# Fewer loads at the end of a decode attention kernel, and another home for the last 64 rows of the down projection

## The chip, the cores and the metric

One Trainium2 chip, one NeuronCore of it. The metric is the device time of one execution in microseconds; lower is better. Each kernel is run several times and the median is given. The profile is one more execution, taken by the hardware profiler; its span runs from the first to the last instruction. Names of engines: PE is TensorE (PEld its weight loads), DVE is VectorE, ACT is ScalarE, POOL is GpSimd, SP is SyncE, which issues nearly all DMAs here.

## The reference

One token of a conditioned transformer block: adaptive layer norm, attention of 32 heads over a cache of 16384 keys each, and a SwiGLU feed-forward layer, all in bfloat16.

```python
# A_x (1,1,640); A_k_cache, A_v_cache (1,32,16384,128); A_wq (640,4096); A_wo (4096,640)
# B_w_gate, B_w_up (640,1728); B_w_down (1728,640); c (1,640); w_mod (640,3840)
def A_ref(x, k, v, wq, wo):
    q = (x @ wq).reshape(1, 1, 32, 128).transpose(0, 2, 1, 3)
    p = softmax(einsum('bhqd,bhkd->bhqk', q, k) * 128 ** -0.5)
    return einsum('bhqk,bhkd->bhqd', p, v).transpose(0, 2, 1, 3).reshape(1, 1, 4096) @ wo

def B_ref(x, w_gate, w_up, w_down):
    return silu(x @ w_gate) * (x @ w_up) @ w_down

sa, ca, ga, sb, cb, gb = split(silu(c) @ w_mod, 6)
x = x + ga * A_ref(layernorm(x) * (1 + ca) + sa, k, v, wq, wo)
out = x + gb * B_ref(layernorm(x) * (1 + cb) + sb, w_gate, w_up, w_down)
```

The two caches are 268 of the 290 MB that are read.

## The kernel before

The 32 heads are worked in 16 pairs (NP = 16). A pair's K is 8 MB, laid out as 128 partitions (two heads times 64) with 256 keys of 128 numbers each; its V likewise. K goes to one of the two slots of `kring`, V to `vbuf`; the V of the last pair (PL = 15) goes to slot 0 of `kring`, because `vbuf` is wanted for wo.

Every operation is entered in a list by `op` or `dma` with the operations that it depends on. Each engine works through its own entries in the order of the list and waits on semaphores for the others. SP issues the DMAs in the order of the list too, and a DMA that has to wait for a free buffer holds back the ones behind it.

For one pair:

- *Scores* (`score` in the loop, `score_end` for the first and last pair): DVE multiplies K by the query (`qbc`) in place, 128x16384 elements at a time, that is half a pair, and folds the 128 products per key in halves to 16 by additions (`fold`). `score` splits the pair by the inner dimension and waits for all of K; `score_end` splits it by keys at `KCUT`, and its two halves wait for the load that holds them.
- *Reduction* (`reduce_mm`, `reduce_end`): 16 matmuls with the identity add up the 16 partial sums of a half into `S_ps`.
- *Softmax*: `largest` (DVE maximum, ACT, and a matmul `mx`), `weigh` (DVE `nb`, then two ACT exponentials into `PZ`). For pair p these are entered within the first half of the scores of pair p + 1; for the last pair they come after its own reduction.
- *PV* (`pv`): 64 matmuls over V into `acc_ps`, copied to `acc_sb` by ACT; `diag` picks each head's diagonal block into `OT_sb`.

`load_k(p + 1)` waits for the reduction of pair p - 1, `load_v(p)` for PV of pair p - 1. Pairs 1 to 14 run in the loop over `step`. The last pair is written out behind it, in this order: V of 15 issued, first half of its scores and reduction, PV of 14, the loads of wo into `vbuf`, `diag` of 14, the second half and reduction, its softmax, the loads of gate, up and down into slot 1 of `kring` (they wait for the last reduction), PV of 15, `diag`, the normalisation (lines 664 to 675, up to `A_sb`), wo (`project`, once for each load of wo: two matmuls for each of 32 row blocks, four column strips of PE side by side), eviction to `wo_row` (line 690), columns (line 696), the second layer norm with the first fifth of gate within it (`gate0`), the rest of gate, the x1 rows (line 743), up, `gu` (line 756) and down (line 773).

In gate and up (`f_gu`, line 721) the weights are the stationary operand: for each of the KC = 5 row chunks k there are 13 operands of 128 columns (a stride of 4 columns in the blocks of `BLOCKS`) and one of 64, for F = 1728 = 13 x 128 + 64. Column j of `gu_col` is thus the input of down for row block j. Down's last 64 rows are loaded as 128 half rows (`wt_v`, the entry `None` in `DOWN`); a matmul with `twice` copies the 64 values of `gu` to 128 partitions, and `gu_half` masks them for the two halves, so that four matmuls of 128 rows do this block.

Of the kernel before, what the change touches and what calls it, by code (L numbers as in the profile page):

```python
# [37 lines left out]
class _Plan:  # L38
# [38 lines left out]
    def op(self, eng, fn, deps=(), name="", chan=None):  # L77
        o = _Op(eng, fn, list(deps), name, len(self.ops), self.loop.get(eng), chan)
        o.sig = chan is not None
        self.ops.append(o)  # L80
        return o

    def dma(self, out_ap, in_ap, key, deps=(), name="", eng="sp", noncontig=False):
        nc = self.nc

        def fn(e, out_ap=out_ap, in_ap=in_ap, noncontig=noncontig):
            if noncontig:
                with nc.allow_non_contiguous_dma(reason="tiny vector layout change"):
# [130 lines left out]
def build(nc, A_x, A_k, A_v, A_wq, A_wo, B_wg, B_wu, B_wd, c_in, w_mod, out):  # L219
    H, S, Dh = A_k.shape[1], A_k.shape[2], A_k.shape[3]  # L220
    D = A_x.shape[2]
    F = B_wg.shape[1]
    assert Dh == 128 and D % 128 == 0 and S == 128 * 128 and H == 32
    KC = D // 128
    NP = H // 2
    T2 = 2 * S // 128
# [4 lines left out]
    NF = 13  # L231

    BLOCKS = [(0, 4, 0), (512, 4, 4), (1024, 4, 8), (1536, 1, 12)]

    DOWN = [(0, 0, 4), (1, 0, 4), (None, 0, 0), (2, 0, 4), (3, 0, 1)]
    FCH = NF + 1
    QW = 32
    QR = 16
    RW = D // 4
# [3 lines left out]
    with es:  # L243
# [5 lines left out]
        def sb(name, shape, dtype):  # L249
            return es.enter_context(nc.sbuf_tensor(name, list(shape), dtype))  # L250
# [13 lines left out]
        wt_v = kb[:, wd0 + NF * D:wd0 + NF * D + D // 2]  # L264

        qbc = sb("qbc", [128, NP, 128], BF16)
        PZ = sb("PZ", [128, NCH, 8], BF16)
# [46 lines left out]
        gu_half = sb("gu_half", [128, 2], BF16)  # L314
        even = sb("even", [128, 2], F32)
        twice = sb("twice", [64, 64, 2], BF16)
# [103 lines left out]
        def f_e32(e):  # L420
            with nc.allow_low_precision(reason="sum of one 1 and zeros"):
                return e.tensor_reduce(out=e32[:], in_=ident[:].rearrange("p (j k) -> p k j", k=32), axis=AX.X, op=ALU.add)
        o_e32 = op(DVE, f_e32, deps=[o_ident], name="e32")
        o_even = op(DVE, lambda e: e.tensor_reduce(
            out=even[:], in_=ident[:].rearrange("p (j k) -> p k j", k=2), axis=AX.X, op=ALU.add), deps=[o_ident], name="even")
        o_twice = op(DVE, lambda e: e.tensor_copy(out=twice[:], in_=ident[0:64, 0:64].unsqueeze(2).broadcast_to([64, 64, 2])), deps=[o_ident], name="twice")
        o_ind = op(DVE, lambda e: e.tensor_copy(out=ind[:], in_=e32[:, 0:1]), deps=[o_e32], name="ind")


# [62 lines left out]
        d_k, d_v = [None] * NP, [None] * NP  # L492
        o_R, o_pv, o_exp, o_nb, o_mx, o_acc, o_ot = ([None] * NP for _ in range(7))
        KCUT = [0, T2 // 2, T2]
        VCUT = [0, 3 * T2 // 4, T2]
        v_at = lambda p: vbuf[:] if p < NP - 1 else kring[:, 0]

        def load_k(p):
            deps = [o_R[p - 2]] if p >= 2 else ([o_mod[1]] if p == 1 else [])
            cuts = KCUT if p in (0, NP - 1) else [0, T2]  # L500
            d_k[p] = [dma(kring[:, p % 2, a:b], k_src(p)[:, a:b], ("k", p % 2, c), deps=deps, name="dma_k%d_%d" % (p, c))
                      for c, (a, b) in enumerate(zip(cuts, cuts[1:]))]

# [63 lines left out]
        def score_end(p, c, between=None):  # L567

            kv = kring[:, p % 2, KCUT[c]:KCUT[c + 1]]
            o = op(DVE, lambda e: e.tensor_tensor(  # L570
                out=kv, in0=kv, in1=qbc[:, p, :].unsqueeze(1).broadcast_to([128, KCUT[c + 1] - KCUT[c], 128]), op=ALU.mult),
                deps=[d_k[p][c]] + o_qev[p // 2], name="mult%d_%d" % (p, c))
            for i, w in enumerate((64, 32, 16)):
                if between and i < 2:
                    between[i]()
                o = op(DVE, lambda e, w=w: e.tensor_tensor(out=kv[:, :, 0:w], in0=kv[:, :, 0:w], in1=kv[:, :, w:2 * w], op=ALU.add),  # L576
                       deps=[o], name="fold%d_%d_%d" % (p, c, w))
            return o
# [31 lines left out]
        def step(p):  # L610
# [2 lines left out]
            o_R[p] = reduce_mm(p, 1, score(p, 1))  # L613
            diag(p - 1)

        load_k(0)
        load_k(1)
        load_v(0)
# [3 lines left out]
        for p in range(1, NP - 1):  # L622
            plan.in_loop(("pe",), "pairs", p - 1, NLOOP)
            if p >= FIRST:
                plan.in_loop(("act", "dve"), "pairs", (p - FIRST) // 2, (NP - 1 - FIRST) // 2)
            load_k(p + 1)
            step(p)
            load_v(p)
        plan.out_of_loop(("pe", "act", "dve"))


# [4 lines left out]
        reduce_end(PL, 0, f0)  # L636
        pv(PL - 1)
        wo_src = A_wo.rearrange("(p k) n -> p k n", p=128)
        WCUT = [0, H // 2, 7 * H // 8, H]
        d_wo = [dma(wo_v[:, a:b, :], wo_src[:, a:b, :], ("wo", a), deps=[o_pv[PL - 1]], name="dma_wo%d" % a) for a, b in zip(WCUT, WCUT[1:])]  # L640
        diag(PL - 1)
        f1 = score_end(PL, 1)
# [9 lines left out]
        d_wu = dma(wu_v, wu_src, "wu", deps=wdeps, name="dma_wu")  # L652
        d_wd = []
        for i, (b, r0, r1) in enumerate(DOWN):
            if b is None:
                dst, src = wt_v, B_wd[NF * 128:F, :].rearrange("q (h n) -> (q h) n", h=2)
            else:
                f0, n, j0 = BLOCKS[b]
                dst, src = wd_v[:, j0 + r0:j0 + r1, :], B_wd[f0:f0 + 128 * n, :].rearrange("(p r) n -> p r n", r=n)[:, r0:r1, :]
            d_wd.append(dma(dst, src, ("wd", i), deps=wdeps, name="dma_wd%d" % i))  # L660


# [45 lines left out]
            deps=[o_ga, o_xf], name="x1")  # L708

        def chunk(j):  # L710
            if j == NF:
                return slice(128 * NF, F), 64
            f0, n, j0 = [b for b in BLOCKS if b[2] <= j < b[2] + b[1]][0]
            return slice(f0 + j - j0, f0 + 128 * n, n), 128

        def f_gu(e, wv, ps_t, src, n, k0, k1):
            last = None
            for k in range(k0, k1):
                for j in range(FCH):
                    cols, w = chunk(j)  # L720
                    last = e.matmul(ps_t[0:w, n * j:n * j + n], lhsT=wv[:, k, cols], rhs=src[:, n * k:n * k + n],  # L721
                                    start=(k == 0 and j == 0), stop=(k == KC - 1 and j == FCH - 1), skip_group_check=True)
            return last
        ab_f = ab[:].rearrange("p k n -> p (k n)")
        o_g0 = []
# [14 lines left out]
        def f_xr(e):  # L740
            last = None
            for r in range(4):
# [10 lines left out]
        o_dg = op(DVE, lambda e: e.tensor_scalar_add(out=dg[:], in0=eg[:], scalar1=1.0), deps=[o_eg], name="dg")  # L753
        o_rg = op(DVE, lambda e: e.reciprocal(out=rg[:], in_=dg[:]), deps=[o_dg], name="rg")
        o_sg = op(DVE, lambda e: e.tensor_tensor(out=sg[:], in0=g_sb[:], in1=rg[:], op=ALU.mult), deps=[o_rg, o_gs], name="sg")
        o_gum = op(DVE, lambda e: e.tensor_tensor(out=gu_col[:], in0=u_ps[:, 0:FCH], in1=sg[:], op=ALU.mult), deps=[o_sg, o_u], name="gu")
        o_tw = op(PE, lambda e: e.matmul(attn_ps[:, 8:9], lhsT=twice[:].rearrange("p q h -> p (q h)"), rhs=gu_col[0:64, NF:FCH], start=True, stop=True),
                  deps=[o_gum, o_twice, o_abf], name="twice_gu")
        o_guh = op(DVE, lambda e: e.tensor_tensor(out=gu_half[:], in0=attn_ps[:, 8:9].broadcast_to([128, 2]), in1=even[:], op=ALU.mult),
                   deps=[o_tw, o_even], name="gu_half")  # L760

        for i, (b, r0, r1) in enumerate(DOWN):

            if b is None:
                work = [(gu_half[:, r // 2:r // 2 + 1], wt_v[:, RW * (r % 2):RW * (r % 2) + RW], r) for r in range(4)]
            else:
                j0 = BLOCKS[b][2]
                work = [(gu_col[:, j:j + 1], wd_v[:, j, RW * r:RW * r + RW], r) for j in range(j0 + r0, j0 + r1) for r in range(4)]

            def f_down(e, i=i, work=work):  # L770
                last = None
                for at, (col, rows, r) in enumerate(work):
                    last = e.matmul(f_ps[32 * r:32 * r + 32, 0:RW], lhsT=wide(col), rhs=rows, start=(i == 0 and at < 4),  # L773
                                    stop=(i == len(DOWN) - 1 and at >= len(work) - 4), tile_position=(0, 32 * r))
# [56 lines left out]
```

## Time and profile before

| | |
|---|---|
| Median of 3 runs | 680.29 us (680.27 to 680.42) |
| The profiled execution | 680.31 us, span 678.6 us |
| Mean granted clock of TensorE | 0.593 of full speed |
| Busy: DVE, PE, ACT, POOL | 512.5, 365.1, 46.7, 0.7 us |
| DMA | 290.58 MB in 6787 packets, mean 428 GB/s |
| Share of 16 DMA engines taken by the queue of SP | 99.2% |
| Chain that ended last, by engine | DMA 53%, DVE 23%, issue 12%, PE 11% |
| Loads in the trace: K of 15, V of 15, wo | 2 of 4096 KB; 6144 and 2048 KB; 2560, 1920 and 640 KB |
| Loads of down | three of 640 KB, one of 160 KB, one of 80 KB (the last 64 rows) |

In the views of the profile a line is an instruction or a group: start and duration in us, engine, line of the kernel, operation, output<-inputs by the program's names, shapes, count, and in brackets the idle time ahead of it and what ended it. In the chain of waits each line is a start, a duration and what that time went to. In the view by stretches the columns are the stretch, its length, the busy time and number of instructions of each engine (PE, PEld, DVE, ACT, POOL), the granted TensorE clock as a share of full speed, the busy share of the DMA engines and GB/s. In the view of DMA issues the last number is the time from issue to landing, a median where there are several. Busy shares are means over stages with different limits; what a step is worth is read from its own stage.

### The profile page before, as it was taken

The numbers are of one execution on the slowest core, as the hardware profiler recorded it, in microseconds if no ns is written. First come the engines' busy times: TensorE is split into PE (matmuls) and PEld (weight loads), VectorE is DVE, ScalarE is ACT, GpSimd is POOL, SyncE is SP. The second block draws the span as 40 slices with busy tenths as digits, with TensorE's granted clock in tenths as the row PEclk, the third lists the DMA queues.
The fourth block names the chain that finished last, engine by engine and source line by source line (L and its number), as shares of the span: only waits on it lengthen the run. The fifth ranks groups of instructions, "written<-read, shape, count | busy, mean of one in ns | idle before, by whom it ended". The sixth has DMA issues, their size and how long they took to land.

```text
span 678.6 us, 5426 instructions
## 1 busy us (share of the span) xinstructions
PE 365.1 (54%) x2076; PEld 146.6 (22%) x2076; DVE 512.5 (76%) x184; ACT 46.7 (7%) x147; POOL 0.7 (0%) x6
## 2 busy tenths in 40 slices
PE   2512285755628174654818365563817475472757
PEld 1101122221212122221302122121212222131326
DVE  2189997959596996959597795959698695999401
ACT  1110000100000000000000010000000000000110
POOL 0000000000000000000000000000000000000000
PEclk9765565565756565565657565565757556575675
DMA  9999999999999999999999999999999999999997
GB/s 374 441 461 433 433 433 430 433 429 433 433 433 437 433 433 433 433 433 433 433 433 433 433 433 433 433 437 433 433 433 433 433 433 433 425 440 418 426 426 303
DMA packets 6787, 290.58 MB, mean 428 GB/s; under 512 B 762, under 2 KB 1020, under 8 KB 1532
## 3 DMA queue, kind: packets, MB, share of 16 engines
q1 hardware_dynamic: 6772, 290.48, 99.2%
q8 instruction: 5, 0.08, 0.0%
q14 instruction: 2, 0.02, 0.0%
q10 hardware_dynamic: 8, 0.00, 0.0%
HBM read 290.47 MB, written 0.00 MB: 428 GB/s over the span
## 4 chain that ended last, share of the span: by engine, by line
DMA 53%; DVE 23%; issue 12%; PE 11%; SPq 0%; DVEq 0%; ACT 0%
DMA kring<-in_A_k_cache_dram 44%; DVE kring L554 9%; PE psb L544 7%; DVE kring L559 6%; DMA kring<-in_B_w_up_dram 4%; DMA vbuf<-in_A_v_cache_dram 4%; DVE kring L564 3%; DVE kring L570 3%; DVE kring L576 2%; PE psb L518 2%; PE psb L584 1%; PE psb L721 0%; PE psb L773 0%; DVE pm L590 0%; DVE nb L598 0%
## 5 line engine op out<-in xcount | busy, mean ns | idle before, releaser
L554 DVE TENSOR_TENSOR kring<-kring,qbc 128x16384 bf16<-128x16384 bf16 x28 | 243.2, 8687 | 96.3 <-DMA kring<-in_A_k_cache_dram 96.3
L544 PE MATMUL psb<-kring,ident 128*128 x448 | 197.5, 607 | 122.1 <-DVE kring L564 122.1
L559 DVE TENSOR_TENSOR kring<-kring 128x8192 bf16<-128x8192 bf16 x28 | 123.7, 4420 | 0.5
L544 PEld LDWEIGHTS psb<-kring,ident 128*128 128x128 bf16 x448 | 53.9, 120 | 249.9 <-issue 249.0
L518 PE MATMUL psb<-vbuf,PZ 128*8 128x512 bf16 x960 | 80.5, 509 | 6.3 <-DMA vbuf<-in_A_v_cache_dram 6.3
L594 PE MATMUL psb<-d,bd_f 128*128 128x64 f32 x32 | 11.0, 446 | 114.6 <-ACT d L592 114.6
L564 DVE TENSOR_TENSOR kring<-kring 128x4096 bf16<-128x4096 bf16 x28 | 64.0, 2285 | 0.5
L570 DVE TENSOR_TENSOR kring<-kring,qbc 128x16384 bf16<-128x16384 bf16 x4 | 34.7, 8686 | 16.0 <-DMA kring<-in_A_k_cache_dram 16.0
L518 PEld LDWEIGHTS psb<-vbuf,PZ 128*8 128x8 bf16 x960 | 26.5, 107 | 65.1 <-issue 48.3
L584 PE MATMUL psb<-kring,ident 128*128 128x128 bf16 x64 | 14.5, 392 | 36.0 <-DVE kring L576 36.0
L594 PEld LDWEIGHTS psb<-d,bd_f 128*128 128x128 f32 x32 | 8.0, 311 | 116.7 <-DVE pm L590 114.5
L576 DVE TENSOR_TENSOR kring<-kring 128x8192 bf16<-128x8192 bf16 (+2 forms) x12 | 31.7, 2644 | 0.3
L533 PEld LDWEIGHTS psb<-sel,acc_sb 128*128 128x128 f32 x128 | 28.5, 310 | 8.5 <-issue 4.3
L533 PE MATMUL psb<-sel,acc_sb 128*128 128x2 f32 x128 | 25.6, 322 | 1.4 <-ACT acc_sb L524 1.4
L524 ACT ACTIVATE acc_sb<-psb 128x512 f32<-128x512 f32 x16 | 9.6, 597 | 216.3 <-PE psb L518 216.3
L602 ACT ACTIVATE PZ<-psb,nb 64x256 bf16<-64x256 f32 x32 | 15.0, 469 | 64.8 <-DVE nb L598 64.6
L584 PEld LDWEIGHTS psb<-kring,ident 128*128 128x128 bf16 x64 | 7.5, 122 | 42.4 <-DVE kring L576 37.2
L592 ACT ACTIVATE d<-negid,pm 128x64 f32<-128x64 f32 x16 | 5.6, 348 | 142.1 <-DVE pm L590 142.1
L477 PE MATMUL psb<-vbuf,h_col 128*128 128x512 bf16 x40 | 10.3, 422 | 7.9 <-DMA vbuf<-in_A_wq_dram 7.9
L537 ACT ACTIVATE OT_sb<-psb 128x2 f32 (+1 forms) x16 | 2.8, 172 | 154.2 <-PE psb L533 154.2
L590 DVE TENSOR_REDUCE pm<-psb 128x1 f32<-128x256 f32 x16 | 6.7, 418 | 5.2 <-PE psb L584 5.2
L702 DVE MEMSET psb<- 128x28 f32 x1 | 0.1, 82 | 9.6 <-ACT qbc L690 9.6
(103 smaller groups left out, 86.8 us busy)
## 6 DMA issues: line engine op xcount, KB each, us to landing
kring<-in_A_k_cache_dram SPq DMA_DIRECT2D x4, 4096.0 KB, 36.7
kring<-in_A_v_cache_dram SPq DMA_DIRECT2D x1, 6144.0 KB, 34.2
vbuf<-in_A_wq_dram SPq DMA_DIRECT2D x1, 5120.0 KB, 25.7
kring<-in_w_mod_dram SPq DMA_DIRECT2D x1, 4800.0 KB, 14.0
vbuf<-in_A_wo_dram SPq DMA_DIRECT2D x1, 2560.0 KB, 18.9
kring<-in_B_w_gate_dram SPq DMA_DIRECT2D x1, 2160.0 KB, 25.1
kring<-in_B_w_up_dram SPq DMA_DIRECT2D x1, 2160.0 KB, 29.9
kring<-in_A_v_cache_dram SPq DMA_DIRECT2D x1, 2048.0 KB, 38.7
```

The costliest lines, as they stand in the source:

```text
L477: last = e.matmul(q_ps[b][:, 0:512], lhsT=h_col[:, k:k + 1].broadcast_to([128, 128]), rhs=wq_v[:, k, g * 512:(g + 1) * 512], start=(k == 0 ...
L518: last = e.matmul(acc_ps[32 * s:32 * s + 8, :], lhsT=PZ[:, j, :], rhs=v_at(p)[:, 4 * j:4 * j + 4, :].rearrange("p t d -> p (t d)"), start= ...
L533: last = e.matmul(OT_ps[:, 0:2], lhsT=acc_sb[:, 128 * i:128 * (i + 1)], rhs=sel[:, i:8:4], start=(i == 0), stop=(i == 3))
L544: last = e.matmul(S_ps[:, 0:T2], lhsT=ident[:], rhs=kring[:, bass.ds(plan.slot(p), 1), :, d].rearrange("p o t -> p (o t)"), start=(d == 0) ...
L554: return e.tensor_tensor(out=kv4, in0=kv4, in1=q4, op=ALU.mult)
L559: o_f = op(DVE, lambda e: e.tensor_tensor(out=kv4[:, :, 0], in0=kv4[:, :, 0], in1=kv4[:, :, 1], op=ALU.add), deps=[o_m], name="fold%d_%d" ...
L564: return op(DVE, lambda e: e.tensor_tensor(out=lo[:, :, 0:QR], in0=lo[:, :, 0:QR], in1=lo[:, :, QR:QW], op=ALU.add), deps=[o_f], name="fol ...
L570: o = op(DVE, lambda e: e.tensor_tensor(out=kv, in0=kv, in1=qbc[:, p, :].unsqueeze(1).broadcast_to([128, KCUT[c + 1] - KCUT[c], 128]), op= ...
L576: o = op(DVE, lambda e, w=w: e.tensor_tensor(out=kv[:, :, 0:w], in0=kv[:, :, 0:w], in1=kv[:, :, w:2 * w], op=ALU.add), deps=[o], name="fol ...
L584: last = e.matmul(S_ps[:, KCUT[c]:KCUT[c + 1]], lhsT=ident[:], rhs=kring[:, p % 2, KCUT[c]:KCUT[c + 1], d], start=(d == 0), stop=(d == 15))
L594: o_mx[p] = op(PE, lambda e: e.matmul(mx_ps[:, 0:64], lhsT=bd_f[:], rhs=d2[:], start=True, stop=True), deps=[o_d2, o_bd1, o_bd2, o_nb[p - ...
L602: o_exp[p] = op(ACT, lambda e, half=half, ps=ps: e.activation(out=PZ[ps, :, 4 * half:4 * half + 4], in_=S_ps[ps, 0:T2].rearrange("p (c i) ...
```

## The change

K of the last pair is loaded in one piece instead of two (both halves of `score_end` of pair 15 now wait for it), V of the last pair in one instead of two, wo in two instead of three (28 and 4 row blocks).

Down's last 64 rows go to a tile of their own, `wt`, of 48 partitions by three blocks, which POOL fills with zeros at the start. Block j holds rows at partitions 0 to n and 32 to 32 + n (`SHORT`: 16, 12 and 4 rows in each of the two places). They are loaded in 24 DMAs of every fourth partition (4, 3 or 1 rows of 1280 bytes), six behind `load_v` of each of pairs 4 to 7, all on one semaphore.

Gate and up take these 64 columns as three operands of 48, 44 and 36 columns per k, which overlap so that the wanted values come out on the partitions where `wt` has its rows; all 15 of them come behind all operands of 128 columns, in gate behind the last four k. `gu_col` is filled with zeros at the start; `gu` writes its 13 full columns, and six small DVE operations write the short pieces. `twice`, `even` and `gu_half` go; down gets 12 matmuls of 48 rows for the short blocks, between its second and third load.

```diff
-    DOWN = [(0, 0, 4), (1, 0, 4), (None, 0, 0), (2, 0, 4), (3, 0, 1)]
-    FCH = NF + 1
+    DOWN = [(0, 0, 4), (1, 0, 4), (2, 0, 4), (3, 0, 1)]
+    SHORT = [(0, 16), (16, 12), (28, 4)]
+    NS = len(SHORT)
+    KT = 48
+    FCH = NF + NS
+    DEALT = 4
...
+        wt = sb("wt", [KT, NS, D], BF16)
...
-        o_even = op(DVE, lambda e: e.tensor_reduce(
-            out=even[:], in_=ident[:].rearrange("p (j k) -> p k j", k=2), axis=AX.X, op=ALU.add), deps=[o_ident], name="even")
-        o_twice = op(DVE, lambda e: e.tensor_copy(out=twice[:], in_=ident[0:64, 0:64].unsqueeze(2).broadcast_to([64, 64, 2])), deps=[o_ident], name="twice")
+        o_wtz = op(POOL, lambda e: e.memset(wt[:].rearrange("p j n -> p (j n)"), 0.0), name="wt0")
+        o_guz = op(POOL, lambda e: e.memset(gu_col[:], 0.0), name="gu0")
...
-        VCUT = [0, 3 * T2 // 4, T2]
+        VCUT = [0, T2]
...
-            cuts = KCUT if p in (0, NP - 1) else [0, T2]
+            cuts = KCUT if p == 0 else [0, T2]
...
-                deps=[d_k[p][c]] + o_qev[p // 2], name="mult%d_%d" % (p, c))
+                deps=[d_k[p][min(c, len(d_k[p]) - 1)]] + o_qev[p // 2], name="mult%d_%d" % (p, c))
...
+        def load_short(at):
+            last = None
+            for j, (f0, n) in enumerate(SHORT):
+                for a in (0, 32):
+                    f = 128 * NF + f0 + a
+                    last = dma(wt[a + at:a + n:4, j, :], B_wd[f + at:f + n:4, :], "wt", deps=[o_wtz], name="dma_wt%d_%d_%d" % (j, a, at))
+            return last
...
             load_v(p)
+            if DEALT <= p < DEALT + 4:
+                d_wt = load_short(p - DEALT)
...
-        WCUT = [0, H // 2, 7 * H // 8, H]
+        WCUT = [0, 7 * H // 8, H]
...
-            for k in range(k0, k1):
-                for j in range(FCH):
-                    cols, w = chunk(j)
-                    last = e.matmul(ps_t[0:w, n * j:n * j + n], lhsT=wv[:, k, cols], rhs=src[:, n * k:n * k + n],
-                                    start=(k == 0 and j == 0), stop=(k == KC - 1 and j == FCH - 1), skip_group_check=True)
+            for k, j in [(k, j) for k in range(k0, k1) for j in range(NF)] + [(k, j) for k in range(KC if k1 == KC else 0) for j in range(NF, FCH)]:
+                w = 128 if j < NF else 32 + SHORT[j - NF][1]
+                last = e.matmul(ps_t[0:w, n * j:n * j + n], lhsT=wv[:, k, chunk(j)], rhs=src[:, n * k:n * k + n],
+                                start=(k == 0 and j == 0), stop=(k == KC - 1 and j == FCH - 1), skip_group_check=True)
...
-        o_gum = op(DVE, lambda e: e.tensor_tensor(out=gu_col[:], in0=u_ps[:, 0:FCH], in1=sg[:], op=ALU.mult), deps=[o_sg, o_u], name="gu")
-        o_tw = op(PE, lambda e: e.matmul(attn_ps[:, 8:9], lhsT=twice[:].rearrange("p q h -> p (q h)"), rhs=gu_col[0:64, NF:FCH], start=True, stop=True),
-                  deps=[o_gum, o_twice, o_abf], name="twice_gu")
-        o_guh = op(DVE, lambda e: e.tensor_tensor(out=gu_half[:], in0=attn_ps[:, 8:9].broadcast_to([128, 2]), in1=even[:], op=ALU.mult),
-                   deps=[o_tw, o_even], name="gu_half")
+        def scale_up(name, a, z, j0, j1):
+            return op(DVE, lambda e: e.tensor_tensor(out=gu_col[a:z, j0:j1], in0=u_ps[a:z, j0:j1], in1=sg[a:z, j0:j1], op=ALU.mult),
+                      deps=[o_sg, o_u, o_guz], name=name)
+        o_gum = scale_up("gu", 0, 128, 0, NF)
+        o_gus = [scale_up("gu%d_%d" % (a, j0), a, a + n, j0, j0 + 1) for a in (0, 32) for j0, (f0, n) in enumerate(SHORT, NF)]
...
+            short = [(gu_col[0:KT, NF + j:NF + j + 1], wt[:, j, RW * r:RW * r + RW], r) for j in range(NS) for r in range(4)]
...
-            prev = op(PE, f_down, deps=[o_gum if b is not None else o_guh, d_wd[i], o_nb[PL]], name="down%d" % i)
+            if i == 2:
+                op(PE, lambda e, work=short: f_down(e, 1, work), deps=o_gus + [d_wt], name="down_short")
+            prev = op(PE, f_down, deps=[o_gum, d_wd[i], o_nb[PL]], name="down%d" % i)
```

More of the change, by code (lines that the diff above doesn't have):

```diff
@@ L263, in build @@
         wd_v = kb[:, wd0:wd0 + NF * D].rearrange("p (k n) -> p k n", k=NF)
-        wt_v = kb[:, wd0 + NF * D:wd0 + NF * D + D // 2]
         qbc = sb("qbc", [128, NP, 128], BF16)
@@ L313, in build @@
         gu_col = sb("gu_col", [128, FCH], BF16)
-        gu_half = sb("gu_half", [128, 2], BF16)
-        even = sb("even", [128, 2], F32)
-        twice = sb("twice", [64, 64, 2], BF16)
+        wt = sb("wt", [KT, NS, D], BF16)
         o_row = sb("o_row", [128, RW], BF16)
@@ L654, in build @@
         for i, (b, r0, r1) in enumerate(DOWN):
[L655 to L659, printed above, removed]
+            f0, n, j0 = BLOCKS[b]
+            dst, src = wd_v[:, j0 + r0:j0 + r1, :], B_wd[f0:f0 + 128 * n, :].rearrange("(p r) n -> p r n", r=n)[:, r0:r1, :]
             d_wd.append(dma(dst, src, ("wd", i), deps=wdeps, name="dma_wd%d" % i))
@@ L710, in chunk @@
         def chunk(j):
-            if j == NF:
-                return slice(128 * NF, F), 64
+            if j >= NF:
+                f0, n = SHORT[j - NF]
+                return slice(128 * NF + f0, 128 * NF + f0 + 32 + n)
             f0, n, j0 = [b for b in BLOCKS if b[2] <= j < b[2] + b[1]][0]
-            return slice(f0 + j - j0, f0 + 128 * n, n), 128
+            return slice(f0 + j - j0, f0 + 128 * n, n)
         def f_gu(e, wv, ps_t, src, n, k0, k1):
             last = None
-            for k in range(k0, k1):
-                for j in range(FCH):
-                    cols, w = chunk(j)
-                    last = e.matmul(ps_t[0:w, n * j:n * j + n], lhsT=wv[:, k, cols], rhs=src[:, n * k:n * k + n],
-                                    start=(k == 0 and j == 0), stop=(k == KC - 1 and j == FCH - 1), skip_group_check=True)
+            for k, j in [(k, j) for k in range(k0, k1) for j in range(NF)] + [(k, j) for k in range(KC if k1 == KC else 0) for j in range(NF, FCH)]:
+                w = 128 if j < NF else 32 + SHORT[j - NF][1]
+                last = e.matmul(ps_t[0:w, n * j:n * j + n], lhsT=wv[:, k, chunk(j)], rhs=src[:, n * k:n * k + n],
+                                start=(k == 0 and j == 0), stop=(k == KC - 1 and j == FCH - 1), skip_group_check=True)
             return last
@@ L755, in build @@
         o_sg = op(DVE, lambda e: e.tensor_tensor(out=sg[:], in0=g_sb[:], in1=rg[:], op=ALU.mult), deps=[o_rg, o_gs], name="sg")
-        o_gum = op(DVE, lambda e: e.tensor_tensor(out=gu_col[:], in0=u_ps[:, 0:FCH], in1=sg[:], op=ALU.mult), deps=[o_sg, o_u], name="gu")
-        o_tw = op(PE, lambda e: e.matmul(attn_ps[:, 8:9], lhsT=twice[:].rearrange("p q h -> p (q h)"), rhs=gu_col[0:64, NF:FCH], start=True, stop=True),
-                  deps=[o_gum, o_twice, o_abf], name="twice_gu")
-        o_guh = op(DVE, lambda e: e.tensor_tensor(out=gu_half[:], in0=attn_ps[:, 8:9].broadcast_to([128, 2]), in1=even[:], op=ALU.mult),
-                   deps=[o_tw, o_even], name="gu_half")
-        for i, (b, r0, r1) in enumerate(DOWN):
[L764 to L768, printed above, removed]
+        def scale_up(name, a, z, j0, j1):
[3 more added lines that the diff above has]
+        o_gus = [scale_up("gu%d_%d" % (a, j0), a, a + n, j0, j0 + 1) for a in (0, 32) for j0, (f0, n) in enumerate(SHORT, NF)]
+        for i, (b, r0, r1) in enumerate(DOWN):
+            j0 = BLOCKS[b][2]
+            work = [(gu_col[:, j:j + 1], wd_v[:, j, RW * r:RW * r + RW], r) for j in range(j0 + r0, j0 + r1) for r in range(4)]
+            short = [(gu_col[0:KT, NF + j:NF + j + 1], wt[:, j, RW * r:RW * r + RW], r) for j in range(NS) for r in range(4)]
             def f_down(e, i=i, work=work):
```

## The prediction

> **What bounds the kernel now.** The profiled execution took 680.31 us (span 678.6, so 1.7 lie outside it); the runs' median is 680.29, so sums against the one hold for the other. I read the page first, then the chain of waits in order of time, the timeline of the last 80 us, the DMA issues there, the granted clock by stretches, and the records of line 721.
>
> ```profile
> DMA  9999999999999999999999999999999999999997
> HBM read 290.47 MB, written 0.00 MB: 428 GB/s over the span
> ```
>
> The DMA engines are full from first to last, so until 660 us the kernel is a stream of bytes; a step before that costs only what it pushes into the tail. The chain's tail:
>
> ```profile
> 628.23 6.57 PE psb L518 x62
> ...
> 636.53 3.50 PE psb L584 x16
> ...
> 640.41 29.88 DMA kring<-in_B_w_up_dram
> ...
> 670.34 3.39 PE psb L721 x70
> ...
> 674.23 2.02 PE psb L773 x50
> ```
>
> V of pair 14 lands at 628.18, PV follows, then the last reduction of pair 15 (line 584) frees the buffer for gate, up and down. The up weights land at 670.30 and up starts at 670.34: that landing ends the last wait. But PE is nearly as late: the x1 rows (line 743) stream until about 669.98 (second set from 669.72, 0.27 long as the first), so the attention side has a slack of only 0.36 us. The steps behind it:
>
> ```profile
> 601.27 8.68 DVE L570 TENSOR_TENSOR kring<-kring,qbc 128x16384 bf16<-128x16384 bf16 x1
> ...
> 618.13 8.68 DVE L570 TENSOR_TENSOR kring<-kring,qbc 128x16384 bf16<-128x16384 bf16 x1
> ...
> 626.85 8.01 DVE L576 TENSOR_TENSOR kring<-kring 128x8192 bf16<-128x8192 bf16 x3
> ...
> 636.39 3.63 PE L584 MATMUL psb<-kring,ident 128*128 128x128 bf16 x16
> ...
> 652.19 0.20 ACT L675 ACTIVATE A_sb<-psb 128x32 bf16<-128x32 f32 x1 [0.90 <-PE psb L673]
> ...
> 653.88 1.65 PE L684 MATMUL psb<-vbuf,A_sb 128*32 128x512 bf16 x32 [1.73 <-DMA vbuf<-in_A_wo_dram]
> 658.39 2.38 PE L684 MATMUL psb<-vbuf,A_sb 128*32 128x512 bf16 x32 [2.87 <-DMA vbuf<-in_A_wo_dram]
> ...
> 660.84 0.77 ACT L690 ACTIVATE qbc<-psb 128x512 f32<-128x512 f32 x2 [8.46 <-PE psb L684]
> ```
>
> DVE starts pair 15 at 601.27, the moment it is free; wo, cut in three, follows its landings (653.74, 658.35, 660.00), with A_sb ready long before, at 652.39. The issues of the first K half alone, then of both halves:
>
> ```profile
> kring<-in_A_k_cache_dram SPq DMA_DIRECT2D x1, 4096.0 KB, 29.1
> kring<-in_A_k_cache_dram SPq DMA_DIRECT2D x2, 4096.0 KB, 33.8
> ```
>
> Issued at 570.04, the first half landed at 599.12. The second, issued at 570.41, took 2 x 33.8 (their median) - 29.1, or 38.4 unrounded, and landed at 608.83.
>
> **K of pair 15 in one load.** DVE's first half now waits for all of it: 608.9, not 601.27, +7.6. Queued behind on DVE are pair 14's maximum and bias and all of pair 15. The block from 601.27 to 634.86 is 33.6 without a hole, so it ends at 642.5. Line 584's first half then runs 625.9 to 629.5 ahead of PV of 14, which slips from 628.23 to 629.5 and still ends before 638. The last reduction slips from 636.39 to 642.5 and ends at 646.2, not 640.04: +6.15. (1.45 of the 7.6 was slack, while PE had PV.) Gate, up and down are issued 6 us later; wo lies in the queue to 660.0 and covers that: nothing. But weights, PV and normalisation of 15 follow the reduction: PV starts at 649.8 (V landed at 647.65), A_sb is done at 658.5.
>
> **wo in two loads.** [...] By 658.5 the first load (28 of 32 blocks, 658.35) is there, so A_sb ends the wait and all 64 matmuls are still to do. Price by the clock. At full clock 32 took 1.65, with eight every 0.27; at half clock eight every 0.53 and 0.73 for the last eight. 64 cost 7 x 0.27 + 0.5 = 2.4 or 7 x 0.53 + 0.73 = 4.5. Which?
>
> ```profile
> 648.00:650.00 2.00, 1.31 (x28) 0.37 (x16) 0.00 (x0) 0.60 (x1) 0.00 (x0) 1.00 0.88 379
> ...
> 654.00:656.00 2.00, 1.53 (x32) 0.68 (x26) 0.00 (x0) 0.00 (x0) 0.00 (x0) 0.66 0.99 422
> 656.00:658.00 2.00, 0.00 (x0) 0.00 (x0) 0.00 (x0) 0.00 (x0) 0.00 (x0) 0.50 1.03 420
> ```
>
> The clock (second to last but one column) changes on a grid of 3.41 us. [...] In the 16 such stretches it stayed for two units when PV went on 1.51 us or more past the rise (11), for one when 1.45 or less (5). Here it rose at 647.82, 4.2 into PV, and lasted to 654.64. On the same grid PV from 649.8 gets it at 654.64, 4.8 in, and PV (then 6.06, not 5.72) goes on 1.2: one unit, to 658.06. A_sb is then at 658.9 and wo runs at half clock to 663.4, eviction at 663.45, not 660.84: +2.6. I take half clock.
>
> **Gate and up.** The records:
>
> ```profile
> L721 PEld LDWEIGHTS psb<-h_col,kring x70: 110/118/134, 670.3 to 673.5; 128*128 128x128 bf16 x65, 128*64 128x64 bf16 x5
> ```
>
> Starts within a k lie 0.033 apart for 128 columns; the one of 64 comes 0.09 late and the next 0.14 later still, so a k takes 0.658, of which 13 x 0.033 = 0.43, and the 64-column operand 0.225. Now 65 full operands run on, then 15 of 48, 44 and 36 columns. Loads of that kind in a row: line 696 has 10 fp32 loads of 128 columns in 2.28, 0.228 each; per column and two bytes that is about 0.04 for these. Ends: 0.033, and 0.14 if each waits for the one before; the fp32 row is nearest, as it is the only unbroken run of ordinary loads. Up: 65 x 0.033 + 0.06 + 0.09 + 15 x 0.04 + 0.2 = 3.1 for 3.39, -0.28. Gate0 loses its narrow operand (-0.14), gate goes from 2.60 to about 2.45 (-0.15): -0.3 together. [...]
>
> **Down's last 64 rows.** Out of the tail go one load (0.21 between its landing and the one before; the last lands at 675.4, needed at 677), gu_half, and twice_gu, which held down back by 0.12. In come 12 matmuls for 4, 8 x 0.033 = +0.27, and six small DVE steps behind gu, 6 x 0.2 = 1.2, against 1.07 of PE work on down's first two blocks: a wait of some 0.15. Behind the waiting matmuls stand down's last two blocks, and the end waits for those. Together +0.3 (0 to 0.6). The 24 early loads cost SP 24 x 0.4 us, six at a time behind load_v, where SP then waits 9 to 10 us for the next release: covered; without that cover, 2.4 us on a K load. The POOL fills are over 100 us early. Of each such load an engine takes a 1280-byte packet: the one of x at 5.63 us pushed its engine's next packet back by 0.05. A load has 4, 3 or 1 rows (eight loads of each), so four engines get 24, 16, 16 and 8 of the 64: one loses 24 x 0.06 = 1.4, two 0.9. K of 15 landed engine by engine from 607.17 to 608.83, on thirteen within 0.7 of the first: 1.4 on an early engine is hidden, 0.9 on the latest is not.
>
> **Sum.** wo +2.6, less gate 0.3, less slack 0.36: up starts 1.95 later, at 672.3 (its weights landed at 670.3). Up -0.28, down +0.3: +2.0, or 682.3.
>
> **Rivals.**
> 1. *Full clock through wo* (0.20). A_sb at 658.5, wo to 661.0: the +0.2 goes into the slack and up again waits for its landing. -0.28 + 0.3 gives 680.3. [...]
> 2. *Late engines* (0.15). The small loads sit on an engine that is already last: K of 15 is 0.9 later and so is every step: 683.2. For it: 0.9 on either of the two latest engines is enough; against it, eleven or more of sixteen have room. [...]
> 3. *Narrow operands one by one* (0.08). At 0.14, 15 cost 1.5 more in gate and in up: 685.3.
> 4. *Full clock in gate and up* (0.07), the other side: the unbroken stream counts as busy and fills one unit before up. Loads at full clock take half (line 533: eight in 0.97, in 2.02 at half). With wo as in rival 1, up falls from 3.1 to 1.7 and down by 0.5: 678.4. It decides if gate keeps PE counted as busy for 3.41 us; against it, 668 to 676 was busy throughout at 0.50.
>
> **Numbers.** Forecast 0.50 (681.7 to 682.9). A measurement here tells 0.2%, 1.36 us, from no change. Slower 0.64: the forecast less 0.06 (operands at 0.033 and no wait in down take off 0.5), rival 2 less 0.03 (at full clock it gives 681.2), and rival 3. Within 0.29: rival 1 and those two parts. Faster 0.07: rival 4. The range, 680.1 to 683.9, takes in rivals 1 and 2 and leaves out 0.15.
>
> **What would show it.** Right: DVE idle 601 to 609, line 584 last from 642.5, wo from 658.5 to 659 as one run of 64 at 0.50, up some 2 us past its landing and 80 operands in 3.1. Wrong: DVE's first product starting before 608, wo at 1.00, up starting at its landing, or a gap in the DMA row after 646.

## The result, and the profile after

Median 680.91 us (680.41 to 682.74, 22 runs), beside 680.47 for the kernel before (680.09 to 680.78, 22 runs): ratio 1.0012, interval 1.0006 to 1.0017. That is slower by 0.44 us, inside the 0.2% that the prediction called no change, and inside its range. But the runs are of two kinds: 12 lie at 680.41 to 680.93, 10 at 681.25 to 682.74. The profiled execution, 680.52 us with a span of 678.4, is of the first kind.

The chain of waits after, in order of time:

```profile
570.05 38.86 DMA kring<-in_A_k_cache_dram
608.91 0.02 issue
608.94 8.69 DVE kring L571
...
642.59 3.66 PE psb L585 x16
...
646.63 23.48 DMA kring<-in_B_w_up_dram
670.11 0.05 issue
670.16 2.96 PE psb L730 x80
...
673.43 2.58 PE psb L780 x48
```

K of pair 15 is now the load that the tail hangs on, and DVE after it; the chain goes over the last reduction (584 before, 585 now) to the landing of the up weights and to up, as before. The page gives DVE 30% of the chain for 23%, DMA 48% for 53%. The timeline of the steps between:

```profile
608.94 8.69 DVE L571 TENSOR_TENSOR kring<-kring,qbc 128x16384 bf16<-128x16384 bf16 x1 [7.43 <-DMA kring<-in_A_k_cache_dram]
...
642.59 3.64 PE L585 MATMUL psb<-kring,ident 128*128 128x128 bf16 x16 [5.84 <-DVE kring L577]
...
649.87 5.54 PE L519 MATMUL psb<-kring,PZ 128*8 128x512 bf16 x64
...
658.28 0.20 ACT L684 ACTIVATE A_sb<-psb 128x32 bf16<-128x32 f32 x1 [0.90 <-PE psb L682]
658.53 2.37 PE L693 MATMUL psb<-vbuf,A_sb 128*32 128x512 bf16 x64 [0.29 <-ACT A_sb L684]
660.96 0.77 ACT L699 ACTIVATE qbc<-psb 128x512 f32<-128x512 f32 x2 [2.49 <-PE psb L693]
...
673.20 0.68 DVE L766 TENSOR_TENSOR gu_col<-psb,sg 128x13 bf16<-128x13 f32 x7 [2.10 <-PE psb L730]
...
673.42 1.25 PE L780 MATMUL psb<-kring,gu_col 128*32 128x160 bf16 x32 [0.32 <-DVE gu_col L766]
...
674.61 0.59 PE L780 MATMUL psb<-wt,gu_col 48*32 48x160 bf16 x12
...
675.13 0.86 PE L780 MATMUL psb<-kring,gu_col 128*32 128x160 bf16 x20
```

DVE waits 7.43 for K; wo is one run of 64 matmuls behind A_sb, but in 2.37, at full clock. In the view by stretches, cut at the 3.41-us units of the clock (columns as in the prediction; the column after POOL's is the granted clock):

```profile
653.78:657.19 3.41, 2.68 (x40) 1.45 (x32) 0.00 (x0) 0.60 (x1) 0.00 (x0) 1.00 0.78 330
657.19:660.60 3.41, 2.26 (x61) 1.43 (x65) 0.48 (x2) 0.37 (x2) 0.00 (x0) 1.00 1.08 454
```

The clock rose at 653.78, 3.9 into PV, and stayed up for three units, to 664.02. The records of line 730 in up:

```profile
L730 PEld LDWEIGHTS psb<-h_col,kring x80: 110/118/130, 670.2 to 672.9; 128*128 128x128 bf16 x65, 128*48 128x48 bf16 x5, 128*44 128x44 bf16 x5, 128*36 128x36 bf16 x5
```

By the chain of waits, up's 80 operands take 2.96 where 70 took 3.39, and down's matmuls 2.58 where they took 2.02.

### The profile page after: what moved, and what is told of

Same layout as the page of the kernel before. It is cut to its first block, busy times and chain, and to the rows that moved or that the text cites. A ratio compares the mean times of both kernels' runs of the same rounds, so it can differ in the third digit from the quotient of the medians.

```text
span 678.4 us, 5505 instructions
## 1 busy us (share of the span) xinstructions
PE 364.1 (54%) x2102; PEld 146.1 (22%) x2103; DVE 512.8 (76%) x187; ACT 46.7 (7%) x147; POOL 2.4 (0%) x8
## 4 chain that ended last, share of the span: by engine, by line
DMA 48%; DVE 30%; issue 12%; PE 9%; SPq 0%; DVEq 0%
DMA kring<-in_A_k_cache_dram 45%; DVE kring L555 10%; PE psb L545 7%; DVE kring L560 6%; DVE kring L571 5%; DVE kring L577 5%; DMA kring<-in_B_w_up_dram 3%; DVE kring L565 3%; PE psb L585 1%; PE psb L730 0%; PE psb L780 0%; DVE pm L591 0%; DVE nb L599 0%; SPq L90 0%; DVEq L191 0%
## 5 line engine op out<-in xcount | busy, mean ns | idle before, releaser
L478 PEld LDWEIGHTS psb<-vbuf,h_col 128*128 128x128 bf16 x40 | 4.3, 113 | 15.6 <-DMA vbuf<-in_A_wq_dram 8.8
```

Source lines behind the costliest of these rows:

```text
L478: last = e.matmul(q_ps[b][:, 0:512], lhsT=h_col[:, k:k + 1].broadcast_to([128, 128]), rhs=wq_v[:, k, g * 512:(g + 1) * 512], start=(k == 0 ...
```

## The experiments

The theory: K in one load pushes PV of 15 up against wo; wo's 64 matmuls all follow A_sb; what they cost is set by the clock, which comes in units of 3.41 us whose phase differs from execution to execution. The rival: something else in the change costs time, such as the cuts of wo and V by themselves, or the early rows. In three series of runs the kernel before took 680.46, 680.54 and 680.37; each difference below is to the one of its own series.

**K of pair 15 in two loads again** (all else changed).

```diff
-            cuts = KCUT if p == 0 else [0, T2]
+            cuts = KCUT if p in (0, NP - 1) else [0, T2]
```

> The changed kernel with K of pair 15 again in two loads; nothing else undone. Theory (late K, then the clock): A_sb is back at about 652.4, wo follows its landings, up starts at the landing of its weights in every run, so the runs lie as close together as those of before (some 0.7 us) and the median is 680.1 to 680.3, 0.2 under before: up 3.39 to 3.1, down +0.1. Rival (the 24 early loads make late engines, and the landings at the end vary): still a median near 680.9 and single runs over 682.

Median 681.92 (681.62 to 682.42), +1.46, ratio 1.0023 [1.0014, 1.0032]. The expectation failed: with K early the kernel is slower. Its timeline and two units of its clock:

```profile
647.64 5.67 PE L519 MATMUL psb<-kring,PZ 128*8 128x512 bf16 x64 [5.27 <-DMA kring<-in_A_v_cache_dram]
...
656.18 0.20 ACT L684 ACTIVATE A_sb<-psb 128x32 bf16<-128x32 f32 x1 [0.90 <-PE psb L682]
658.37 4.04 PE L693 MATMUL psb<-vbuf,A_sb 128*32 128x512 bf16 x64 [2.23 <-DMA vbuf<-in_A_wo_dram]
```
```profile
655.24:658.65 3.41, 0.47 (x10) 0.32 (x14) 0.48 (x2) 0.24 (x2) 0.00 (x0) 1.00 0.85 355
658.65:662.06 3.41, 3.41 (x60) 2.10 (x56) 0.00 (x0) 0.00 (x0) 0.00 (x0) 0.50 1.04 444
```

A_sb is ready 2 us earlier, but 28 of wo's 32 blocks are one load, which lands at 658.24. In the wait PE has 0.47 us of work in a unit, the clock falls at 658.65, and wo takes 4.04; up starts at 671.35, late by 1.3.

**The same with wo in three loads** (K in two).

```diff
-        WCUT = [0, 7 * H // 8, H]
+        WCUT = [0, H // 2, 7 * H // 8, H]
```

> The changed kernel with K of pair 15 again in two loads and wo again in three (16, 12 and 4 row blocks); V in one load, gate, up and down as changed. Theory (the large wo load is what costs in the run with K alone split: A_sb was ready at 656.4, yet all 64 matmuls stood behind the load that landed at 658.3, and the clock had fallen by then): with a cut at 16 blocks half of wo runs before 658, what is left after it is 32 matmuls, 2.4 at half clock; eviction by 660.8, up at its landing; median 680.0 to 680.3, below both kernels. Rival (V in one load, or something else that the split of K brings, costs the 1.45 us): 681.6 to 682.3, as in the run with K alone split.

680.65 (680.29 to 680.87), +0.11, ratio 1.0002 [0.9993, 1.0011].

```profile
656.12 1.28 PE L693 MATMUL psb<-vbuf,A_sb 128*32 128x512 bf16 x32 [0.29 <-ACT A_sb L684]
...
658.29 2.33 PE L693 MATMUL psb<-vbuf,A_sb 128*32 128x512 bf16 x32 [0.89 <-DMA vbuf<-in_A_wo_dram]
```

Half of wo is done before the second load; 32 matmuls take 1.28 at full clock (the prediction's 1.65 has the fall at 654.64 in it) and 2.33 at half, what 64 take at full. So 1.35 of the 1.46 was the large load of wo, not V. The hope of 680.0 to 680.3, below both kernels, was a miss; what down takes back (below) is the reason.

**PE kept busy, K in two loads** (wo in two). 13 groups of four matmuls whose result nobody reads, behind PV, `diag` and the normalisation of 15.

```diff
+        def keep(n):
+            def f_keep(e):
+                for j in range(n):
+                    for s in range(4):
+                        last = e.matmul(f_ps[32 * s:32 * s + 8, :], lhsT=PZ[:, j, :], rhs=..., tile_position=(0, 32 * s))
+                return last
+            op(PE, f_keep, deps=[o_nb[PL], d_v[PL][-1]], name="keep")
         pv(PL)
+        keep(2)
         diag(PL)
+        keep(3)
...
+        keep(8)
```

> The changed kernel with K of pair 15 in two loads and groups of matmuls that nobody reads (13 groups of 4, 512 columns each) put behind PV, diag and the normalisation of pair 15, so that PE stays busy until wo lands at 658.3. Theory (the clock alone decides what wo costs behind its landing): wo's 64 matmuls in 2.4 us at full clock, eviction by 660.9, up at its landing, 680.2 to 680.6, no run above 681.2. Rival (the split of K costs by something other than the clock): 681.6 to 682.3, as in the run with K alone split.

680.71 (680.14 to 681.15), +0.17 [0.9994, 1.0012]. The clock stays up from 652.51 to 666.16:

```profile
658.73 2.37 PE L706 MATMUL psb<-vbuf,A_sb 128*32 128x512 bf16 x64 [0.22 <-DMA vbuf<-in_A_wo_dram]
```

wo still waits for the large load (landed at 658.60), but the price of the wait went: 1.29 of the 1.46 was the clock.

**PE kept busy, on the changed kernel** (6 groups: 2, 3 and 1).

> The changed kernel with PE kept at work between PV of pair 15 and wo: groups of four matmuls over V into a bank that is not read, two behind PV, three behind its diagonal, one behind the matmul ahead of A_sb. Theory: the clock then stays full into wo in every run, A_sb comes at 658.4 to 659.9, wo takes 2.4, and the runs lie at 680.4 to 681.0 with none above 681.3. Should the fill itself cost at half clock, at most 0.4 more. Rival (early loads): the spread to 682.7 stays.

680.49 (679.99 to 680.75), +0.03, ratio 1.000 [0.9991, 1.0009]. The kernel does strictly more work and is 0.4 faster; the second kind of run is gone. In the unit in which wo begins PE now has 3.08 for the 2.26 above:

```profile
656.53:659.95 3.42, 3.08 (x64) 1.72 (x68) 0.48 (x2) 0.37 (x2) 0.00 (x0) 1.00 0.98 408
```

**The kernel before with only K of pair 15 in one load.**

> The kernel of before with only K of pair 15 in one load. Theory: A_sb at 658.5; where the clock is full through wo the eviction comes at 661 and the time is that of before (680.4), where it is half it comes at 663.4 and up starts some 2.3 late: runs spread from 680.4 to 682.9, median 680.7 to 681.5, wider than the changed kernel, since gate has no 0.3 to give. Rival (early loads): as before, 680.1 to 680.8, for there are none in this kernel.

680.44, ratio 1.0008 [0.9999, 1.0017], in two kinds: nine runs at 680.07 to 680.54, three at 682.24 to 682.99. The late K alone brings the second kind; with the clock up it costs nothing:

```profile
657.87 0.20 ACT L675 ACTIVATE A_sb<-psb 128x32 bf16<-128x32 f32 x1 [0.90 <-PE psb L673]
658.12 2.37 PE L684 MATMUL psb<-vbuf,A_sb 128*32 128x512 bf16 x64 [0.28 <-ACT A_sb L675]
```

wo is one run here too, although it is loaded in three pieces: A_sb comes long after the first of them, and the second lands (658.24) before its matmuls are due. No profile shows one of the three slow runs.

**Only wo in three loads, K in one.**

> The changed kernel with only wo again in three loads (16, 12 and 4 blocks); K in one load. Theory: A_sb comes at 658.3 to 658.5, when 28 blocks have landed anyway, so the cut of wo has nothing to hide: as the changed kernel, 680.9, with single runs to 682.7, in which the clock falls ahead of wo. Rival (the cut of wo costs whatever K does): 680.0 to 680.4 and no run above 681.

680.88 (680.49 to 682.95; five of 11 over 682), +0.34, ratio 1.0016 [1.0007, 1.0025]: the median is that of the changed kernel. With A_sb ready at 658.56 in the profile and the second load landed at 658.68, the cut of wo has next to nothing to hide.

**The changed kernel again**, for its spread and for a profile of the second kind.

> The changed kernel once more, beside the other three on one chip. Both theories: median 680.7 to 681.2 and single runs up to 682.7. If the profiled run falls in the upper part, theory: wo at half clock (PEclk 0.50 from 658 to 663), eviction at 663 to 664 and up starting 1.5 to 2 us behind the landing of its weights; rival: up starting at its landing, which itself is late.

680.91, +0.45, ratio 1.0015 [1.0007, 1.0024]; six of 11 runs at 680.15 to 680.91, one at 681.33, four at 682.43 to 682.73. Two more single executions:

> The changed kernel once more, to find a profile of one of its runs near 682.5. Theory: if the time is 682 or more, wo's 64 matmuls take over 4 us and the granted clock is 0.5 in that stretch; if it is under 681, 2.4 at full clock. Rival: the slow runs lose their time elsewhere, with wo at 2.4.

> As the look before: 682 or more goes with wo over 4 us at half clock, under 681 with 2.4 at full clock.

680.35 and 681.28. From the unit in which wo begins, the execution of 680.35:

```profile
656.21:659.62 3.41, 1.93 (x45) 1.35 (x48) 0.48 (x2) 0.37 (x2) 0.00 (x0) 1.00 1.00 419
659.62:663.03 3.41, 2.53 (x39) 2.03 (x31) 0.11 (x2) 0.77 (x2) 0.00 (x0) 1.00 1.01 430
```

and the execution of 681.28, by stretches and in the timeline:

```profile
656.35:659.76 3.41, 1.82 (x42) 1.32 (x44) 0.48 (x2) 0.37 (x2) 0.00 (x0) 1.00 0.99 413
659.76:663.17 3.41, 2.55 (x41) 1.34 (x34) 0.11 (x2) 0.77 (x2) 0.00 (x0) 0.50 1.00 425
```
```profile
658.64 3.45 PE L693 MATMUL psb<-vbuf,A_sb 128*32 128x512 bf16 x64 [0.71 <-DMA vbuf<-in_A_wo_dram]
...
671.00 2.92 PE L730 MATMUL psb<-h_col,kring 128*128 128x1 bf16 x80
```

The two differ by 0.11 us of PE work in a unit. With 1.93 the clock stays up and wo takes 2.37; with 1.82 it falls in the middle of wo, which takes 3.45, and up starts 0.66 behind its landing (670.34). In both, wo starts when its first load has landed, not when A_sb is ready: 658.15 after 657.93 in the one, 658.51 after 658.17 in the other. Of that unit's work wo has 1.34 in the one and 1.12 in the other, so here the merged load, landing late, probably took part in the fall. The runs between 681.2 and 681.9 (seven of 35 of the changed kernel) may be of this kind; of the 23 with K late and wo in three loads none lies there, and eight lie above 682.

No profile shows a run of the changed kernel over 682. What such a run would be if the clock had fallen ahead of wo, the next run tests.

**A longer hole between PV and wo.** Line 678 (`on_f`) is done six times, one behind the other.

```diff
-        o_on = op(DVE, lambda e: e.tensor_tensor(out=on_f[:], ...), deps=[o_rl] + o_ot, name="on")
+        again = []
+        for _ in range(6):
+            o_on = op(DVE, lambda e: e.tensor_tensor(out=on_f[:], ...), deps=[o_rl] + o_ot + again, name="on")
+            again = [o_on]
```

> The changed kernel with the product of line 678 (on_f) done six times, one after the other, instead of once: PE has 1.1 to 1.2 us more without work between PV of 15 and wo. Theory (the runs of 682 and more are those in which the clock falls in that hole): A_sb at 659.5; with the clock up, wo to 662 and 681.5 to 681.9; with the clock down, 683.3 to 684; half of the runs or more are of the second kind, against 3 in 10 without the hole. Rival (the slow runs have another cause): all runs shift by 0.8 alike and the share stays at 3 in 10.

682.56 (682.25 to 684.14, 6 runs), ratio 1.0036 [1.0024, 1.0048]. No run lies at 681.5 to 681.9. Of its fastest run, 682.25, the profile:

```profile
655.69:659.10 3.41, 1.11 (x15) 0.83 (x19) 1.44 (x7) 0.37 (x2) 0.00 (x0) 1.00 0.96 402
659.10:662.51 3.41, 3.41 (x60) 1.97 (x56) 0.00 (x0) 0.00 (x0) 0.00 (x0) 0.50 1.01 431
```

1.11 us of work in the unit, and wo takes 4.04. So even the fastest run is of the half-clock kind, which the rival (all runs later by 0.8, 3 in 10 slow) does not allow. Five of the six lie 0.7 to 1.0 below the 683.3 to 684 that was expected: in the profiled one the clock rose early, at 652.27, PV ended early, A_sb was ready at 658.79, not 659.5, and wo's own work raised the clock again at 662.51, before wo's end. The run shows that a fall ahead of wo makes times over 682; it does not show why the clock falls there in the changed kernel.

**All loads as before, gate, up and down as changed.**

```diff
-        VCUT = [0, T2]
+        VCUT = [0, 3 * T2 // 4, T2]
```

and the two edits of K and wo above.

> The changed kernel with all loads of the last pair and wo cut as before the change (K and V in two loads, wo in three): what is left of the change is gate, up and down with the early rows. By the prediction this part is -0.28 (up) and +0.3 (down): 680.5, the time of the kernel before, with no run above 681.2. Rival (the early rows on four engines cost by themselves, as the 6 early loads of consecutive rows did with 0.5): 681.0 or more, the up weights landing 0.4 later than before.

680.70 (680.51 to 680.84), +0.33, ratio 1.0005 [0.9996, 1.0014]. One kind of run. Between the two expectations: the up weights landed at 670.64 in its profile, 0.34 later than in the profile before; where that time went is told below (late engines). One unit of its granted clock:

```profile
649.03:652.45 3.42, 1.83 (x21) 1.14 (x13) 0.49 (x2) 0.77 (x2) 0.00 (x0) 1.00 1.01 433
```

Here the clock rose 5.75 into PV (643.28 to 649.73) and fell after one unit. wo then ran at half clock throughout, and that cost nothing, as it follows its landings.

**Down's early rows in six loads of consecutive rows**, all behind `load_v` of pair 4 (with the fill of 6 groups).

```diff
-                    last = dma(wt[a + at:a + n:4, j, :], B_wd[f + at:f + n:4, :], ...)
+                    last = dma(wt[a:a + n, j, :], B_wd[f:f + n, :], ...) if at == 0 else None
```

> The changed kernel with the fill of the earlier run (6 groups, 680.49) and down's last 64 rows in 6 early loads of consecutive rows (two each of 16, 12 and 4 rows, so up to 16 DMA engines take one row of a load) instead of 24 loads on four engines. Theory (four engines lose 0.5 to 1.4 us and the latest of all sets when K, wo and the up weights have landed): K of 15 lands 0.1 to 0.3 earlier than 608.9, up weights 0.1 to 0.2 earlier, 680.2 to 680.4. Rival (the four engines have room): as with the fill alone, 680.5.

681.06 (680.80 to 681.42), +0.52 where the fill alone had +0.03. The expectation had the sign wrong. The first product of pair 15, here and then with the fill alone:

```profile
609.74 8.69 DVE L571 TENSOR_TENSOR kring<-kring,qbc 128x16384 bf16<-128x16384 bf16 x1 [7.41 <-DMA kring<-in_A_k_cache_dram]
```
```profile
609.00 8.69 DVE L571 TENSOR_TENSOR kring<-kring,qbc 128x16384 bf16<-128x16384 bf16 x1 [7.41 <-DMA kring<-in_A_k_cache_dram]
```

K lands 0.74 later, the last of the up weights 0.71 later (670.89, 670.18). The stream loses it where the rows are: against the profile before, and counted from the landing of K of pair 5, the next V lands 0.71 late and the K behind it 0.99, and no later K or V loses any more. Some twenty packets of 64 KB beside the rows took 2.6 to 3.4 us there instead of 2.42, on top of the rows' own 0.06 each. Whether that comes from the consecutive rows or from six loads at one place was not separated.

## Why the prediction was right, and where it was not

**K's lateness: right, to 0.1 us.** Forecast 608.9, 642.5, 649.8 and 658.5 for DVE's start, the last reduction, PV and A_sb; measured 608.94, 642.59, 649.87 and 658.48. The shift of gate's and up's issues was covered by wo's bytes, as said: the DMA row has no gap, and the up weights landed at 670.11.

**"I take half clock": the step that failed.** +2.0 was forecast and +0.44 measured; a time clearly slower had 0.64, and no telling change 0.29. The profiled execution and the median are the case of rival 1, which had 0.20, with two of the listed signs of being wrong: wo at 1.00, and up starting at its landing. The measured time lies in the range only because the range took in that rival. The price for full clock was right (680.3, against 680.52 profiled). The case of half clock exists too, in somewhat less than half of the runs (10 of 22, at 681.25 to 682.74 where 681.7 to 682.9 was said), but four of these ten lie below 681.7: the clock can also fall within wo, as in the execution of 681.28, and the prediction had no such case.

Three parts of the working on the clock were wrong.

- It counted on the grid of the profile before. The phase is another in each execution: the clock rises at 653.78, 653.47, 652.79 and 652.93 in four of the changed kernel.
- It put the rise 4.8 into PV. That PV needs so long was the author's estimate, which no run shows, and the 0.20 of rival 1 stood on it. In the profile before the 16 rises lie 1.86 (at 169.95) to 5.93 (at 634.16) into a PV, eight of them less than 3.41; ahead of each lies a unit with 3.41 of PE work, PV's and the reduction's together. In the nine profiles with K late the clock rose 2.55 to 4.44 into PV (3.91 in the profiled execution). Nor was the unit full in every run: with the hole the clock rose after a unit with 3.12 of PE work.
- It let only PV count towards keeping the clock. After the rise at 653.78 PV went on for 1.6, which by the prediction's own border gives two units, to 660.60. The third unit came from the work of wo itself, which makes up 2.07 of the 2.26 in the second.

What keeps the clock is known only in part. Among the second units, of the tail of `diag`, the normalisation and wo, those with 1.93 of PE work or more kept it and those with 1.82 or less let it fall (1.82, 1.56, 1.11, 0.47). In the one with 1.82, of the execution of 681.28, PE was idle for 0.89 at most at a time, and the clock fell at 659.76 with PE at work from 658.64. With other kinds of work in the unit more was not enough: 2.53 with the matmuls of line 705 did not keep it (below), nor did 2.71 in the unit from 634.16 of the profile before (the end of PV, `diag` of 14 and the start of the last reduction). So a first unit with 1.2 of PV and 1.05 of `diag`, the one of the prediction's grid, is not settled by any row here.

Nor is a late rise simply bad or an early one good. Without the fill and with K late, the rises at 2.55 (with the hole) and 2.84 into PV led to a fall before wo's end, and those at 3.03 to 3.91 kept the clock up to it. With all loads as before a rise at 5.75 lasted one unit, as the prediction's border has it. Whether the five runs over 682 had an early rise or a late one, as the prediction had it, stays open: none of them has a profile.

**From wo to up: right.** The sum was: eviction's delay against 660.84, less 0.3 for gate, less 0.36 of slack, gives up's delay against 670.34. For the execution of 681.28 (eviction 662.13) that is 670.97, measured 671.00; with K split (662.47) 671.31 and 671.35; with the hole (662.95) 671.79 and 671.83.

**wo in two loads, for which the sum has no cost: nearly right beside the late K, wrong as a rule.** With K late the cut does not move the median (680.88 with three loads), though the merged load set the start of wo in the execution of 681.28; with A_sb ready at 656.4 the missing cut costs 1.35. The change paired two things that hide each other: without the late K, the uncut wo was its dearest part.

**Up, gate, down: right in sum, by errors that cancel.** By the chain, up fell by 0.43, not 0.28: the narrow operands start 33 to 42 ns apart, as taken, but going over to them cost less than the 0.15 allowed. The seven writes of `gu_col` took 0.68, a tenth of a us each instead of 0.2, and held nothing up; the path from up's end to down is 0.31 instead of 0.50 without `twice_gu`. Down's matmuls took 0.56 more, against +0.3 for down together with what is around it. By the parts: -0.43 - 0.19 + 0.56 = -0.06, forecast +0.02. From the landing of the up weights to the span's end it is the same 8.3 us in four kernels: 678.6 - 670.30 before, 678.4 - 670.11 after, 678.4 - 670.09 with K in two and wo in three, 678.9 - 670.64 with all loads as before. That is why no version came clearly below the kernel before: what up and the path save, down takes back.

Down's 0.56 is not a wait. Four of its matmuls start every 0.13. Eight more are 0.27. The rest is mostly two steps of 0.27 instead of 0.13, one where PE goes over to the short blocks of 48 rows and one where it comes back. They are no waits for the late loads, for they are the same in the run with the hole, where the third load had landed at 674.72, two us ahead:

```profile
676.27 0.59 PE L783 MATMUL psb<-wt,gu_col 48*32 48x160 bf16 x12
676.79 0.86 PE L783 MATMUL psb<-kring,gu_col 128*32 128x160 bf16 x20
```

What makes the step longer was not tested.

**Late engines (rival 2): the right mechanism, in part of the runs and at most 0.6.** In the packet records after, the 16 rows of each of the last three groups lie back to back on four of the 16 engines, 6, 4, 4 and 2 of them, 0.058 apart (the second group from 277.85, the fourth from 355.73). The early rows land behind V of pairs 4 to 7, so a loss must show between the landings of K of pair 5 (221.74 before) and K of pair 9 (376.54). The only two profiles without early rows take 154.80 and 154.81 us for that stretch. Of the eleven profiles with the 24 loads four take 154.81 to 154.83, and seven 154.93 to 155.42. Most of it is lost at K of pairs 8 and 9, which come behind the third and fourth group of rows. K of pair 9 in the chains of the executions of 680.35 and 681.28:

```profile
337.75 38.85 DMA kring<-in_A_k_cache_dram
```
```profile
337.60 39.34 DMA kring<-in_A_k_cache_dram
```

So the same kernel loses nothing in one execution and 0.54 in another, up to 0.62 where 0.9 was allowed for; that the rows sit on the latest engine in the one and not in the other is likely, but the trace does not name the engines. The kernel with all loads as before loses 0.50 there, which is more than the 0.34 by which its up weights land late. The up weights landed at 669.95 to 670.64 in the profiles with the 24 loads.

**The sum of 0.44**, then: the 12 runs of the first kind have a median of 680.61, 0.14 over before, a size that the rows can explain; the rest comes from the 10 slower runs.

## What to carry to other kernels

Before merging two loads, ask not only when the last byte lands but how many matmuls become one burst behind it, and at which clock that burst runs: here the same 64 matmuls cost 2.37 or 4.04. Work on the granted clock by units of the whole tail, count the burst's own work too, and treat the phase as unknown: try every phase, not the one of the profile at hand. Where a burst stands near the border, expect two kinds of run and look at the spread, not the median alone. When a kernel is a stream of bytes to its last load, time saved on PE ahead of that load returns as waiting: gate's 0.3 became 0.24 of idle time ahead of up.

## What the runs showed of the hardware that was not expected

- In units of 3.41 us made of the same kinds of matmul (`diag`, normalisation, wo), 1.82 of PE work let the clock fall and 1.93 kept it. The kind matters as well: 1.46 of PV alone kept it (unit from 559.07 in the profile before) and 1.40 did not (unit from 326.96), while 2.53 in the unit from 659.62 in the run of 680.35, 1.5 of it the ten fp32 matmuls of line 705, did not keep it (it fell at 663.03).
- Those ten matmuls of 128 strided fp32 columns took 2.36 at full clock (661.78 after) and 2.36 at half (662.95 in the execution of 681.28). A doubled clock did not speed up that part.
- Extra matmuls made a kernel faster: 24 that nobody reads took the median from 0.45 over the kernel before to 0.03.
- The same 64 rows cost the stream 1.0 us in the one profile with six loads of consecutive rows at one place, and 0 to 0.6 us in the eleven profiles with 24 small loads at four places.
